# Moving one batch's input loads and folds to later steps of a fused FFT-filter and gated-FFN kernel

## The chip, the cores and the metric

The kernel runs on one core of one Trainium2 chip. Five engines work side by side, each in the order of its own instruction list: TensorE (PE) multiplies matrices, VectorE (DVE) and ScalarE (ACT) work element by element and take results out of PSUM, the accumulator memory, GpSimd (POOL) works element by element on SBUF, the on-chip memory, and SyncE (SP) issues transfers. POOL and ACT can issue transfers too. The metric is device time in microseconds (us); lower is better.

## The reference, cut to what matters

```python
X = np.fft.rfft(x, axis=1)                 # x: 8 batches, 3008 rows, 256 columns
Y = X * (filt_r + 1j * filt_i)[None]
y = np.fft.irfft(Y, n=3008, axis=1)
t = y.reshape(8 * 3008, 256)
out = (np.maximum(t @ w_gate, 0) * (t @ w_val)) @ w_out    # 256 -> 1536 -> 256
```

Each batch is Fourier transformed along its rows, multiplied by a filter, transformed back, and every row then goes through a gated feed-forward layer.

## The kernel before, in words

**The two halves.** The transform is split by 3008 = 94 x 32 into stages of small matmuls. For batches 2 to 7, one batch b goes through this chain:

1. *Chunk loads* (`load_chunk`). The batch's input comes in four chunks j = 0 to 3, each into its own part `XP[j]` of the tiles `XF`. One chunk is six transfers: four of 96 KB and two of 256 KB. They are issued by SP (`nc.sync`) or by POOL (`nc.gpsimd`); a POOL load is preceded by `hold_gpsimd`, a small copy that makes POOL wait for the feed-forward work of its step.
2. *Folds* (`fold_chunk`). Six POOL instructions per chunk form sums and differences, in place in `XP[j]`.
3. *`tiled_a`*. 32 matmuls per chunk into `psF`, copied to `asb` by ACT and DVE and stored by SP to the DRAM buffer `Abuf`.
4. *`load_at_tiled`*. SP loads the whole stage back in another order, into the tile `at`.
5. *Forward blocks* (`fwd`, `product`, `add`). Six blocks per batch, in three pairs: matmuls into `psX`, products with the two filter tables on DVE (`tt`, `uu`), and sums of these on POOL (`pp`).
6. *Inverse* (`inv`). One per pair: matmuls into `psD`, copied to `dsb`, stored by SP to the DRAM buffer `Dbuf`.
7. *`load_d`* brings it back as `dCb`, and `item_c` makes from it the rows `yT` that the feed-forward layer reads.

The feed-forward half is the main loop: 47 blocks of 512 rows, with 12 steps each. A step of `gv` makes one of the 12 hidden slices (two matmuls each into `psV` and `psG`, a copy to `vsb` by ACT, a product by DVE), and `o_part` runs four matmuls of the previous block's output into `psO`. ACT copies these to `osb`, and SP stores them.

**What sets the order.** The order is written out by hand. Step s = 12k + ft is pass ft of block k. The dictionary `side` holds for each step the transform work done in it, and each engine and queue carries out its share in that order. For batch b, `end` is the step its times are counted from: 51 for batch 1, 123 for batch 2, 195 for batch 3, 267 for batch 4. Batch 2 has its `tiled_a` at steps 51, 56, 61, 66, its `load_at_tiled` at 70, its forward pairs at 79, 92 and 105, its adds from one to eight steps behind each of these, its inverses at 90, 103 and 116, its `load_d` at 121 and its first `item_c` at 128. Batch 3 has its `tiled_a` at 123, 128, 133 and 138 and its first forward pair at 151. Batch 1's `load_d` is at step 50.

**The lines that matter.** The lists `loads` and `folds` give the steps of the four chunk loads and the four folds of a batch; batch 2 has its own lists, and the others take theirs from `end`. For batch 3, these come to 53, 59, 78, 101 for the loads and 65, 72, 88, 114 for the folds. The condition in `next_x` says which chunks SP loads. It sends chunks 2 and 3 of batch 2 and chunks 0 and 1 of batch 3 to SP, the rest to POOL.

In the profile, chunk loads are lines 333 and 337, folds 346 to 351, `tiled_a` 360 (matmuls), 367 (copies) and 370 (stores), `load_at_tiled` 378, `fwd` 396, `product` 413, `add` 423 and 424, `inv` 436, its stores 453, `load_d` 481, `item_c` 503, the feed-forward matmuls 520 and 541, and output stores 565.

Of the kernel before, what the change touches and what calls it, by code (L numbers as in the profile page):

```python
# [116 lines left out]
def kernel(  # L117
# [138 lines left out]
    def hold_gpsimd(tile_):  # L256

        scr = sb.tile([128, 8], FP32, tag="scr", bufs=2)
        nc.gpsimd.tensor_copy(scr[:tile_.shape[0]], tile_)  # L259
# [68 lines left out]
    def load_chunk(b, j, eng):  # L328

        xp = XP[j]  # L330
        for q in range(4):
            r, o = 32 * q, 8 * q + 2 * j
            eng.dma_start(xp[r:r + 24, 0:4:2, :],  # L333
                              _ap(x, (b * N1 * N2 + o) * D,
                                  [[N2 * D, 24], [47 * N2 * D, 2], [1, 512]]))
        for i in range(2):
            eng.dma_start(xp[:, 2 * i + 1, :],
                              _ap(x, ((b * N1 + 46 + 47 * i) * N2 + 2 * j) * D,
                                  [[8 * D, 4], [-N2 * D, 32], [1, 512]]))

    def fold_chunk(b, j):

        xp = XP[j]
        t = fs.tile([128, 2, 512], FP32, tag="fold", bufs=1, name="fold")
        tt = nc.gpsimd.tensor_tensor
        tt(t, xp[:, 0:2], xp[:, 2:4], op=ALU.add)  # L346
        tt(xp[:, 2:4], xp[:, 0:2], xp[:, 2:4], op=ALU.subtract)  # L347
        tt(xp[:, 1], xp[:, 2], xp[:, 3], op=ALU.add)
        tt(xp[:, 2], xp[:, 2], xp[:, 3], op=ALU.subtract)
        tt(xp[:, 0], t[:, 0], t[:, 1], op=ALU.add)  # L350
        tt(xp[:, 3], t[:, 0], t[:, 1], op=ALU.subtract)
        fold[b, j] = (xp[:, 0], xp[:, 3], xp[:, 1], xp[:, 2])

    def tiled_a(b, j):

        banks = [bank("psF", 2, D) for _ in range(4)]
        for c in range(4):
            for q in range(4):
                r = 32 * q
                nc.tensor.matmul(banks[q][32 * c:32 * c + 32], WF[r:r + 24, c, :],  # L360
                                 fold[b, j][c][r:r + 24], start=True, stop=True,
                                 tile_position=(r, 32 * c))
        asf = sb.tile([128, NC2 * D], BF16, tag="asb", bufs=3, name="asb")
        asf = asf.rearrange("p (n q d) -> p n q d", n=2, d=D)
        for q in range(4):
            copy = nc.scalar.copy if q % 2 == 0 else nc.vector.tensor_copy
            copy(asf[:, :, q, :], banks[q])  # L367
            done(banks[q])
        for c in range(4):
            nc.sync.dma_start(_ap(Abuf[b], ((48 * (c % 2) + 24 * (1 - c // 2)) * N2 + 8 * j) * D,  # L370
                                  [[N2 * D, 24], [1, 8 * D]]),
                              asf[32 * c:32 * c + 24])

    def load_at_tiled(b):

        ats[b] = sb.tile([128, NG, D], BF16, tag="at", bufs=1, name="at")
        for rr in range(4):
            nc.sync.dma_start(ats[b][32 * rr:32 * rr + 32],
                              _ap(Abuf[b], (48 * (rr % 2) + 24 * (rr // 2)) * N2 * D,
                                  [[D, 32], [N2 * D, 24], [1, D]]))  # L380
# [6 lines left out]
    def fwd(b, i):  # L387

        for e in range(2):
            psXs[b, i, e] = bank("psX", 2, D)  # L390
            left[b, i, e] = 2
        for r in range(2):
            for c in range(4):
                for e in range(2):
                    j = 4 * i + c
                    nc.tensor.matmul(psXs[b, i, e][32 * c:32 * c + 32, r],  # L396
                                     F2[64 * e:64 * e + 64, j, 32 * r:32 * r + 32],
                                     ats[b][64 * e:64 * e + 64, j, :] if b > 1 else ats[b][64 * e:64 * e + 64, :, j, :],
                                     start=True, stop=True, tile_position=(64 * e, 32 * c))

    def product(b, i, e, k, pool=False):

        psX = psXs[b, i, e]
        pool_, bufs, dt = (fs, 3, FP32) if b else (pro, 8, BF16)
        p = pool_.tile([128, 2, D], dt, tag=("tt", "uu")[k], bufs=bufs, name=("tt", "uu")[k])
        filt = (Ftr, Fti)[k][:, 2 * i + e, :]
        filt = dataclasses.replace(filt, ap=[list(filt.ap[0]), [0, 2], list(filt.ap[1])])
        if pool:
            xs = pro.tile([128, 2, D], FP32, tag="xs", bufs=3)
            nc.scalar.copy(xs, psX)  # L410
            nc.gpsimd.tensor_tensor(p, xs, filt, op=ALU.mult)
        else:
            nc.vector.tensor_tensor(p, psX, filt, op=ALU.mult)  # L413
        tus[b, i, e, k] = p
        left[b, i, e] -= 1
        if not left[b, i, e]:
            done(psX)

    def add(b, i, e):

        tt, uu = (tus.pop((b, i, e, k)) for k in range(2))
        p = tus[b, i, e, 0] = fs.tile([128, 2, D], BF16, tag="pp", bufs=6, name="pp")
        nc.gpsimd.tensor_tensor(p[:, 0], tt[:, 0], uu[:, 1], op=ALU.subtract)  # L423
        nc.gpsimd.tensor_tensor(p[:, 1], tt[:, 1], uu[:, 0], op=ALU.add)  # L424
# [50 lines left out]
    def load_d(b):  # L475

        for z in range(NZ):
            i = 8 * (NZ * b + z) % 48
            dCs[b, z] = dCb[:NROW, i:i + 8, :]
            for e in range(2):  # L480
                nc.sync.dma_start(dCs[b, z][48 * e:48 * e + 48],
                                  _ap(Dbuf[b], (64 * e + 16 * z) * NG * D,
                                      [[D, 48], [48 * D, 8], [1, D]]))
# [166 lines left out]
    def at_step(s, f):  # L650
        side.setdefault(s, []).append(f)
# [4 lines left out]
    for b in range(1, B):  # L656
        end = (b * S // W - 1) * NFT + C_AT[0] - 5
        starts, gap = ((-37, -25, -13), 4) if b == 1 else ((-44, -31, -18), 5)
        if b > 1:
            loads, folds = (((6, 12, 20, 30), (22, 34, 46, 46)) if b == 2 else  # L660
                            ([end - 72 + v for v in (-70, -64, -45, -22)], [end - 72 + v for v in (-58, -51, -35, -9)]))
            for j, e in enumerate((-72, -67, -62, -57)):
                def next_x(b=b, j=j):
                    if b == 2 and j > 1 or b == 3 and j < 2:
                        return load_chunk(b, j, nc.sync)
                    hold_gpsimd(prods[-1][:, 0:8])
                    load_chunk(b, j, nc.gpsimd)
                at_step(loads[j], next_x)
                at_step(folds[j], lambda b=b, j=j: fold_chunk(b, j))
                at_step(end + e, lambda b=b, j=j: tiled_a(b, j))  # L670
            at_step(end + e + 4, lambda b=b: load_at_tiled(b))
        for z, l in enumerate(starts):
            for i in (2 * z, 2 * z + 1):
                at_step(end + l, lambda b=b, i=i: fwd(b, i))
                for h in range(4):
                    s = end + l + i % 2 * gap + h
                    at_step(s, lambda b=b, i=i, h=h: product(b, i, h // 2, h % 2))
                    if h % 2:
                        at_step(s, lambda b=b, i=i, h=h: add(b, i, h // 2))

            def back(b=b, z=z, s=end + l + 6 + gap):
                rest = inv(b, z)
                if b == 1:
                    rest()
                else:
                    at_step(s + 1, rest)
            at_step(end + l + 6 + gap, back)
        at_step(end - (1 if b == 1 else 2), lambda b=b: load_d(b))
# [43 lines left out]
```

## Time and profile before

| | |
|---|---|
| Median of 3 runs | 880.95 us (879.96 to 882.09) |
| Profiled execution | 881.05 us |
| Its span, first to last instruction | 879.3 us |
| Busy in the span | PE 98%, DVE 66%, ACT 57%, POOL 54% |
| DMA | 101.62 MB, mean 116 GB/s |
| Granted PE clock, mean of the span | 0.994 of full |

The profile shows one execution. In its rows, a group is named by its source line, its engine, its operation and "output<-input"; "SPq" and "POOLq" are the issue queues of SP and POOL. A timeline row gives the start, the time from there to the end of the last of its instructions, and the count; the part in brackets is the time the engine stood idle before it and what ended that idle time. In an issue row the time is that of issuing, not of moving the data. A row of waits gives the total, how often, and the longest. PE is in-order and its instructions overlap a little, so that starts are a better guide than lengths. A granted clock of 1.00 is full speed, 0.50 half.

### The profile page before, as it was taken

Reading aid. Unit: us, or ns where it says so; the run is one execution under the profiler, and the core shown is the slowest. Engines: PE = TensorE matmul, PEld = TensorE weight load, DVE = VectorE, ACT = ScalarE, POOL = GpSimd, SP = SyncE. Lnnn points to the kernel's source line nnn. Section 1 sums busy time; section 2 is a strip of 40 time slices with the busy share of each in tenths; the row PEclk is TensorE's granted clock in tenths of the full one; section 3 lists DMA queues with packets and bytes.
Section 4 is the critical chain, followed back from the end, with each engine's and each line's share of the span. In section 5 each row is a group of like instructions: output and inputs, shape, how many; then the busy total and the mean of one; then the engine's idle time right before and its main releaser. Section 6 shows DMA issues by size and latency. Waiting matters only on the chain.

```text
span 879.3 us, 20548 instructions
## 1 busy us (share of the span) xinstructions
PE 860.3 (98%) x7709; PEld 500.1 (57%) x7709; DVE 581.9 (66%) x860; ACT 496.8 (57%) x903; POOL 471.2 (54%) x515
## 2 busy tenths in 40 slices
PE   8899999699999999999999999999999999999997
PEld 3345655365556565566655556555655565666665
DVE  3788865387665885577755777657865578655553
ACT  4775566255655556655655555555555555555553
POOL 7837895665677756868549576487660032100001
PEclk9999999799999999999999999999999999999999
DMA  9796364724467246562377433874444522511111
GB/s 234 182 191 141 103 137 136 164 57 101 120 184 140 70 98 151 165 142 56 96 188 171 97 89 90 205 151 103 83 110 114 121 54 60 123 36 35 38 32 54
DMA packets 103262, 101.62 MB, mean 116 GB/s; under 512 B 22411, under 2 KB 90539, under 8 KB 102394
## 3 DMA queue, kind: packets, MB, share of 16 engines
q1 hardware_dynamic: 82970, 76.78, 35.7%
q0 software_dynamic: 19792, 22.74, 12.1%
q8 instruction: 61, 1.00, 0.5%
q10 hardware_dynamic: 400, 0.79, 0.3%
q14 instruction: 39, 0.32, 0.1%
HBM read 58.23 MB, written 45.88 MB: 118 GB/s over the span
## 4 chain that ended last, share of the span: by engine, by line
PE 94%; DMA 3%; DVE 1%; ACT 1%; POOL 1%; issue 0%; SPq 0%; DVEq 0%
PE psV L520 28%; PE psG L520 27%; PE psO L541 27%; PE psF L360 3%; PE psY L503 3%; PE psA L267 2%; PE psD L436 2%; DMA XF<-in_x_dram 2%; PE psX L396 1%; DMA at<-Abuf 1%; DVE tt L413 0%; POOL out_dram L565 0%; DMA Abuf<-asb 0%; ACT AS L445 0%; DVE at L294 0%
## 5 line engine op out<-in xcount | busy, mean ns | idle before, releaser
L525 DVE SCALAR_TENSOR_TENSOR prod<-psG,vsb 128x512 bf16<-128x512 f32 x564 | 388.8, 691 | 237.7 <-ACT vsb L523 231.0
L523 ACT CAST vsb<-psV 128x512 bf16<-128x512 f32 x564 | 332.0, 589 | 234.0 <-PE psV L520 223.9
L541 PE MATMUL psO<-WoT,prod 128*128 128x256 bf16 x2256 | 336.9, 273 | 0.0
L520 PE MATMUL psV<-yT,WvT 128*128 128x512 bf16 x1128 | 336.8, 380 | 0.0
L520 PE MATMUL psG<-yT,WgT 128*128 128x512 bf16 x1128 | 336.2, 380 | 0.0
L541 PEld LDWEIGHTS <-prod 128*128 128x128 bf16 x2256 | 220.9, 98 | 144.1 <-issue 1.1
L520 PEld LDWEIGHTS <-WgT 128*128 128x128 bf16 x1128 | 110.2, 98 | 134.3 <-issue 1.1
L423 POOL TENSOR_TENSOR pp<-tt,uu 128x256 bf16<-128x256 f32 x84 | 61.1, 727 | 182.7 <-DVE uu L413 105.3
L520 PEld LDWEIGHTS <-WvT 128*128 128x128 bf16 x1128 | 100.4, 98 | 33.7 <-issue 22.0
L509 ACT CAST yT<-psY 128x512 bf16<-128x512 f32 x93 | 54.7, 588 | 42.8 <-PE psY L503 42.5
L413 DVE TENSOR_TENSOR tt<-psX,Ftr 128x512 f32<-128x512 f32 (+1 forms) x96 | 65.2, 684 | 11.2 <-PE psX L396 9.6
L554 ACT COPY osb<-psO 128x512 f32<-128x512 f32 x92 | 53.9, 586 | 23.8 <-PE psO L541 22.4
L565 POOL DMA_DIRECT2D out_dram<-osb x5 | 2.6, 536 | 119.4 <-ACT osb L554 119.4
L346 POOL TENSOR_TENSOR fold<-XF 128x1024 f32<-128x1024 f32 x24 | 56.4, 2352 | 11.1 <-DMA Abuf<-asb 9.4
L424 POOL TENSOR_TENSOR pp<-tt,uu 128x256 bf16<-128x256 f32 x84 | 61.0, 726 | 0.0
L413 DVE TENSOR_TENSOR uu<-psX,Fti 128x512 f32<-128x512 f32 (+1 forms) x88 | 59.9, 681 | 0.0
L347 POOL TENSOR_TENSOR XF<-XF 128x1024 f32<-128x1024 f32 x24 | 56.4, 2351 | 1.9
L333 POOL DMA_DIRECT2D XF<-in_x_dram x80 | 48.4, 609 | 1.9 <-issue 1.4
L367 ACT CAST asb<-psF 128x512 bf16<-128x512 f32 x48 | 25.8, 589 | 34.5 <-PE psF L360 34.5
L367 DVE CAST asb<-psF 128x512 bf16<-128x512 f32 x48 | 30.9, 686 | 18.2 <-PE psF L360 18.2
L259 POOL CAST scr<-prod 128x8 f32<-128x8 bf16 x20 | 3.8, 190 | 71.2 <-DVE prod L525 59.1
L503 PEld LDWEIGHTS <-dCb 96*128 96x128 bf16 (+1 forms) x604 | 33.3, 98 | 10.3 <-issue 6.8
(69 smaller groups left out, 483.1 us busy)
## 6 DMA issues: line engine op xcount, KB each, us to landing
Dbuf<-dsb SPq DMA_DIRECT2D x84, 128.0 KB
dCb<-Dbuf SPq DMA_DIRECT2D x56, 192.0 KB
XF<-in_x_dram POOLq DMA_DIRECT2D x40, 256.0 KB, 8.0
Abuf<-asb SPq DMA_DIRECT2D x96, 96.0 KB
at<-Abuf SPq DMA_DIRECT2D x24, 384.0 KB
XF<-in_x_dram POOLq DMA_DIRECT2D x80, 96.0 KB, 5.4
XF<-in_x_dram SPq DMA_DIRECT2D x28, 256.0 KB
out_dram<-osb SPq DMA_DIRECT2D x69, 94.0 KB
```

The costliest lines, as they stand in the source:

```text
L346: tt(t, xp[:, 0:2], xp[:, 2:4], op=ALU.add)
L347: tt(xp[:, 2:4], xp[:, 0:2], xp[:, 2:4], op=ALU.subtract)
L367: copy(asf[:, :, q, :], banks[q])
L413: nc.vector.tensor_tensor(p, psX, filt, op=ALU.mult)
L423: nc.gpsimd.tensor_tensor(p[:, 0], tt[:, 0], uu[:, 1], op=ALU.subtract)
L424: nc.gpsimd.tensor_tensor(p[:, 1], tt[:, 1], uu[:, 0], op=ALU.add)
L503: nc.tensor.matmul(psY[:, o:o + w], dCs[b, n2 // 8][:, n2 % 8, h * 128:(h + 1) * 128], M1[:, 1, n1:n1 + w] if b == 0 else M1[:NROW, 0, n1: ...
L509: nc.scalar.copy(dst, psY)
L520: nc.tensor.matmul(pt[:, :W], w[:, h, ft * 128:(ft + 1) * 128], yt[:, h, :], start=(h == 0), stop=(h == 1))
L523: nc.scalar.copy(vsb, psV[:, :W])
L525: nc.vector.scalar_tensor_tensor(prod, in0=psG[:, :W], scalar=0.0, in1=vsb, op0=ALU.max, op1=ALU.mult)
L541: nc.tensor.matmul(psO[:, t % 2], prods[ft][:, t * 128:(t + 1) * 128], WoT[:, ft, :], start=(ft == 0), stop=(ft == NFT - 1))
```

## The change

For batch 3, the steps of the chunk loads become 78, 87, 98, 110 in place of 53, 59, 78, 101. Those of the folds become 88, 101, 114, 122 in place of 65, 72, 88, 114. SP now loads chunks 1, 2 and 3 of batch 3, and POOL chunk 0; before, SP loaded 0 and 1, and POOL 2 and 3. Other batches keep their steps and their queues.

```diff
         if b > 1:
             loads, folds = (((6, 12, 20, 30), (22, 34, 46, 46)) if b == 2 else
+                            ((78, 87, 98, 110), (88, 101, 114, 122)) if b == 3 else
                             ([end - 72 + v for v in (-70, -64, -45, -22)], [end - 72 + v for v in (-58, -51, -35, -9)]))
             for j, e in enumerate((-72, -67, -62, -57)):
                 def next_x(b=b, j=j):
-                    if b == 2 and j > 1 or b == 3 and j < 2:
+                    if b == 2 and j > 1 or b == 3 and j > 0:
                         return load_chunk(b, j, nc.sync)
                     hold_gpsimd(prods[-1][:, 0:8])
                     load_chunk(b, j, nc.gpsimd)
```

## The prediction

> **What bounds the kernel now.** I read the page first, then TensorE's waits, the chain around the longest of them, and a table by stage. A "step" is one pass of the main loop, number 12k + ft.
>
> ```profile
> span 879.3 us, 20548 instructions
> PE 860.3 (98%) x7709; PEld 500.1 (57%) x7709; DVE 581.9 (66%) x860; ACT 496.8 (57%) x903; POOL 471.2 (54%) x515
> PE 94%; DMA 3%; DVE 1%; ACT 1%; POOL 1%; issue 0%; SPq 0%; DVEq 0%
> ```
>
> TensorE (PE) is busy for 98% of the span and carries 94% of the chain. A change that touches no matmul can only pay, or cost, where PE stands still or runs slowly. Its waits are few:
>
> ```profile
> PE psX L396 <- DMA at<-Abuf: 7.3, 2, 4.1
> PE psA L267 <- DMA XF<-in_x_dram: 3.1, 3, 1.6
> ```
>
> The second row is the start of the program. The first is in the middle, and it is in the stretch that the change edits:
>
> ```profile
> 161.64 0.60 PE L541 MATMUL psO<-WoT,prod 128*128 128x256 bf16 x4
> 165.46 0.39 PE L396 MATMUL psX<-at,F 64*32 64x256 bf16 x1 [3.22 <-DMA at<-Abuf]
> 169.94 1.05 PE L396 MATMUL psX<-at,F 64*32 64x256 bf16 x31 [4.09 <-DMA at<-Abuf]
> 170.92 1.04 PE L520 MATMUL psV<-yT,WvT 128*128 128x512 bf16 x2
> 175.99 0.59 PE L520 MATMUL psV<-yT,WvT 128*128 128x512 bf16 x2
> ```
>
> This is step 79, batch 2's first forward blocks, waiting for `at` (the batch's stage-A result, loaded back from DRAM at step 70). The wait is 3.22 + 4.09 = 7.31 us, and behind it the same pair of matmuls takes 1.04 where it later takes 0.59. What that is worth together is read from the same stretch of four batches, first `tiled_a` to first inverse; columns are the stretch, its length, busy times of PE, PEld, DVE, ACT and POOL, granted PE clock, DMA share, GB/s:
>
> ```profile
> 120.14:188.09 67.95, 60.64 (x518) 33.94 (x526) 36.82 (x56) 33.15 (x60) 43.73 (x38) 0.92 0.58 137
> 235.84:293.42 57.58, 57.58 (x520) 32.89 (x528) 36.71 (x56) 33.08 (x60) 38.44 (x42) 1.00 0.63 154
> 341.13:398.69 57.56, 57.56 (x519) 32.83 (x526) 36.73 (x56) 33.07 (x60) 38.43 (x42) 1.00 0.67 159
> 446.49:504.04 57.55, 57.55 (x519) 32.82 (x526) 36.73 (x56) 33.04 (x60) 38.40 (x42) 1.00 0.66 159
> ```
>
> Batches 3, 4 and 5 need 57.55 to 57.58 us for the same matmuls at clock 1.00; batch 2 needs 67.95 at 0.92. The excess is 67.95 - 57.58 = 10.37 us: 7.31 of standing still and 3.06 of slow clock. It is the only excess of its kind.
>
> **Why `at` is late.** SP's queue, batch 2 and then batch 3, and DMA by single microseconds (the last two columns are share and GB/s):
>
> ```profile
> 131.57 2.13 SPq L333 DMA_DIRECT2D XF<-in_x_dram  x4
> 133.76 1.19 SPq L337 DMA_DIRECT2D XF<-in_x_dram  x2
> 137.24 6.11 SPq L565 DMA_DIRECT2D out_dram<-osb  x4
> 143.52 1.59 SPq L333 DMA_DIRECT2D XF<-in_x_dram  x4
> 145.16 1.19 SPq L337 DMA_DIRECT2D XF<-in_x_dram  x2
> 155.29 1.54 SPq L370 DMA_DIRECT2D Abuf<-asb  x4
> 158.90 2.93 SPq L378 DMA_DIRECT2D at<-Abuf  x4
> ...
> 261.99 1.52 SPq L370 DMA_DIRECT2D Abuf<-asb  x4
> 265.90 2.55 SPq L378 DMA_DIRECT2D at<-Abuf  x4
> ...
> SPq L565 <- DMA XF<-in_x_dram: 9.4, 4, 2.7
> ...
> 143.64 1.07 PE psF L360 x32
> 259.39 1.07 PE psF L360 x32
> ...
> 159.00:160.00 1.00, 1.00 (x8) 0.68 (x7) 0.57 (x1) 0.72 (x2) 0.92 (x2) 1.00 0.06 19
> 160.44 9.37 DMA at<-Abuf
> 275.00:276.00 1.00, 1.00 (x8) 0.54 (x6) 0.69 (x1) 0.72 (x3) 0.00 (x0) 1.00 0.78 157
> 276.00:277.00 1.00, 1.00 (x8) 0.69 (x7) 0.53 (x1) 0.44 (x1) 0.00 (x0) 1.00 0.24 79
> ```
>
> In batch 3 the last Abuf stores are issued 261.99 - 259.39 = 2.60 us after the last `tiled_a` and `at` 265.90 - 259.39 = 6.51 us after it. In batch 2 these are 155.29 - 143.64 = 11.65 and 158.90 - 143.64 = 15.26: 9 us later. The two XF rows are batch 3's chunks 0 and 1 (steps 53 and 59). They put 12 issues (3.4 and 2.8 us) into SP's queue, and the output stores behind them wait another 9.4 us for XF transfers. With everything in order on SP, the last Abuf stores and `at` inherit that. In batch 3 the next batch's chunks are issued by POOL in the same steps, and nothing is late.
>
> **The change, part by part.** (a) *Two SP loads leave steps 53 and 59.* SP then carries in this stretch what it carries in batch 3. `at` should go out at 143.64 + 6.51 = 150.15. Its flight: 158.90 to 160.44 + 9.37 = 169.81 is 10.9 us here; in batch 3 the transfer fades in the 275 and 276 rows, some 10.1 to 10.9 after its issue. So it lands at 160.3 to 161.1, against PE's readiness at about 161.64 + 0.43 = 162.07. I take the stall as gone with 1 to 1.8 us to spare: -10.37 us. Bounds: the whole 10.37, or, if SP still is some 3 us late from `load_d` of batch 1, a wait of about 2 us that stays, with no slow clock worth naming: -8.
>
> On the slow part, the Trainium skill ("TensorE: Matmul & The Clock Gate", Part 1) says that an idle window of about 3.4 us halves the clock and about 3.4 us of busy time restores it. By that the slow part is worth an estimated 1.7 us and the time would be about 872; the trace has 3.06, which decides.
>
> (b) *POOL at step 78.* It issued chunk 2 there and now issues chunk 0, with the same hold and the same six transfers: 0. Its load at step 101 goes, about 4 us of POOL. Rows for it and the folds:
>
> ```profile
> 186.71 2.35 POOL L346 TENSOR_TENSOR fold<-XF 128x1024 f32<-128x1024 f32 x1
> 195.37 1.27 POOL L351 TENSOR_TENSOR XF<-fold 128x512 f32<-128x512 f32 x1
> 204.86 0.72 POOL L424 TENSOR_TENSOR pp<-tt,uu 128x256 bf16<-128x256 f32 x1
> 213.56 0.72 POOL L423 TENSOR_TENSOR pp<-tt,uu 128x256 bf16<-128x256 f32 x1 [4.07 <-PE psG L520]
> 220.34 0.73 POOL L423 TENSOR_TENSOR pp<-tt,uu 128x256 bf16<-128x256 f32 x1 [2.46 <-DVE uu L413]
> 222.94 0.73 POOL L423 TENSOR_TENSOR pp<-tt,uu 128x256 bf16<-128x256 f32 x1 [1.19 <-DVE uu L413]
> 225.52 0.64 PE L436 MATMUL psD<-pp,I2t 32*64 32x256 bf16 x32
> 240.16 0.19 POOL L259 CAST scr<-prod 128x8 f32<-128x8 bf16 x1 [5.94 <-DVE prod L525]
> 277.23 0.19 POOL L259 CAST scr<-prod 128x8 f32<-128x8 bf16 x1 [3.50 <-DVE prod L525]
> ```
>
> (c) *Folds.* One fold is six instructions, 186.71 to 195.37 + 1.27: 9.9 us. All times from here on are on the clock of before. Step 88 keeps a fold, of another chunk. Step 101's is new: it would run 205.6 to 215.5 between the adds of pairs 2 and 3, so the first add of pair 3 slides from 213.56 by 2 us; an add pair takes 1.4 us and the third waits for DVE until 220.34, so POOL has caught up there, well before the inverse at 225.52: 0. Step 114 keeps one. Step 122's is new: 234.2 to 244.2, holding batch 4's first POOL load back from 240.16 by 4 us; POOL has 3.5 us idle ahead of 277.23 and more between batch 3's adds: 0. The two folds taken away at steps 65 and 72 covered nothing.
>
> (d) *SP loads at steps 87, 98, 110.* Each is 2.8 to 3.4 us of issue, plus up to the 6.11 us in which the stores behind it hung. They come some 16 us apart where the two of before came 12 apart. Behind them stand output stores, the Dbuf stores and `load_d`:
>
> ```profile
> 229.16 1.72 SPq L453 DMA_DIRECT2D Dbuf<-dsb  x4
> 233.13 6.68 SPq L481 DMA_DIRECT2D dCb<-Dbuf  x8
> ...
> 244.52 0.42 PE L503 MATMUL psY<-M,dCb 96*128 96x8 bf16 x7
> ...
> 121.60 4.03 SPq L481 DMA_DIRECT2D dCb<-Dbuf  x8
> L503 PEld LDWEIGHTS <-dCb x192: 95/97/152, 128.8 to 388.0; 96*128 96x128 bf16 x182, 128*128 128x128 bf16 x10
> ```
>
> Step 110 is at about 216 (counting steps of 1.3 us back from 225.52), so the last Dbuf stores have 13 us for the load's 3.4 + 6.1: on time. If not, batch 1's `dCb` was read 128.8 - 121.60 = 7.2 us after its issue, so `load_d` may slip 244.52 - 233.13 - 7.2 = 4.2 us unseen. I take 0; as a bound, a slip like the 9 us above, less 3.5 and 4.2, costs about 1.5 us.
>
> **Sum.** PE's own order of instructions is the same in both kernels. The profiled execution is 881.05 us (span 879.3 plus 1.75 around it); 881.05 - 10.37 = 870.7. That execution stands 0.1 above the median of 880.95, so I forecast 870.6. About 0.2% (1.8 us) can be told from no change.
>
> **Rivals.** (1) *Part of the wait stays.* SP is not quite on time, or `at` flies longer than 11 us. The spare time of 1 to 1.8 us speaks for it, three later batches without a wait against. Gain 6 to 8: 873 to 875.
> (2) *Bytes, not the queue.* If `at` were late because the 16 DMA engines were full, moving the issue would mend little: about 881. The 159 row speaks against it: with `at` still unissued, the engines were 0.06 busy. The Trainium skill ("DMA: Bandwidth & Descriptors", Issuing engines are not separate DMA queues) says that a choice of issuing engine saves only sequencer time, usually a small share; that row shows a case where the sequencer's place is what is short.
> (3) *The new SP loads make `dCb` late,* as in (d): 872 to 873; at twice that slip, with slow clock, some 877.
> (4) *Slower: POOL stalls in front of the adds.* The fold of chunk 1 at step 101 stands ahead of pair 3's adds in POOL's order. If its load has not landed, POOL waits and the inverse of step 116 with it. Fold starts up to about 209 cost nothing (four add pairs of 1.4 us behind it end before 225.5); each later microsecond stalls PE, with 3 us of slow clock on top. It takes a stall of 7.3 us, so a fold start near 217, to eat the gain, and more to be slower: 883 for a start at 219. Step 87 is at about 183.5, so the load would have to take 33 us; the longest wait behind an SP load here cleared by 143.35, 11.8 us after its 131.57 issue.
>
> **How the numbers follow.** Full gain 0.78 (own range 869.5 to 872); (1) 0.08; (2) 0.03; (3) 0.05; (4) and anything slower 0.06. Faster is full, (1) and (3): 0.91; same 0.03; slower 0.06. The range 869.3 to 874.0 takes in the full gain, a spread of a microsecond as between the runs, and most of (1) and (3).
>
> **What would show it.** Right: no wait of psX on `at` at step 79, which starts near 162; clock 1.00 there; the stretch from batch 2's first `tiled_a` to its first inverse near 57.6; `at` issued near 150; all later stages at their old lengths, about 10.4 earlier. Wrong: a wait of psX above 1 us; psD waiting for POOL at steps 103 or 116; psY waiting for `dCb` at step 128; or a batch other than 2 with a stretch above 58.

## The result

The changed kernel takes 872.42 us (median of 6 runs, 871.88 to 874.61) against 880.74 us for the kernel before (6 runs, 878.59 to 882.09). The ratio is 0.9911, 95% interval 0.9894 to 0.9927: 8.3 us, or 0.9%, faster. The profiled execution took 872.1 us, its span 870.0.

From TensorE's waits in the changed kernel, which fill seven rows, the longest and the only one of psX (in the views of this part, rows that the text does not need are left out):

```profile
PE psA L267 <- DMA XF<-in_x_dram: 1.6, 3, 0.8
...
PE psX L396 <- DVE at L294: 0.8, 1, 0.8
```

The row that carried the prediction, psX waiting for the transfer `at<-Abuf`, is gone. All seven belong to the start of the program, before the main loop. The table by stage, with the same columns as before, for the stretch from first `tiled_a` to first inverse of batches 2 and 3:

```profile
120.14:177.72 57.58, 57.13 (x504) 32.81 (x510) 36.82 (x56) 33.05 (x60) 24.48 (x26) 1.00 0.61 137
225.47:283.05 57.58, 57.16 (x506) 32.88 (x512) 36.71 (x56) 33.08 (x60) 46.43 (x48) 1.00 0.64 155
```

Batch 2 now needs 57.58 us where it needed 67.95, at clock 1.00 where it had 0.92. (This trace lacks some matmul records, so PE's busy time reads a little low.) SP's queue shows why, in rows that answer to those of steps 61 to 70 before:

```profile
146.38 1.53 SPq L370 DMA_DIRECT2D Abuf<-asb  x4
149.31 2.94 SPq L378 DMA_DIRECT2D at<-Abuf  x4
171.74 3.43 SPq L333 DMA_DIRECT2D XF<-in_x_dram  x4
218.91 1.72 SPq L453 DMA_DIRECT2D Dbuf<-dsb  x4
222.90 6.53 SPq L481 DMA_DIRECT2D dCb<-Dbuf  x8
```

The last Abuf stores go out at 146.38 in place of 155.29, and `at` at 149.31 in place of 158.90. The last `tiled_a` starts at 143.77 in this execution, so `at` is 5.54 us behind it; before it was 15.26. The loads now stand behind `at`, from 171.74 on. The last Dbuf stores and `load_d` come 10.25 us earlier than before, as the rest of the program behind batch 2's stall does.

### The profile page after: what moved, and what is told of

Same layout as the page of the kernel before. It is cut to its first block, busy times and chain, and to the rows that moved or that the text cites. A ratio compares the mean times of both kernels' runs of the same rounds, so it can differ in the third digit from the quotient of the medians.

```text
span 870.0 us, 20431 instructions
## 1 busy us (share of the span) xinstructions
PE 850.7 (98%) x7587; PEld 498.9 (57%) x7709; DVE 581.9 (67%) x860; ACT 496.7 (57%) x903; POOL 467.0 (54%) x508
## 4 chain that ended last, share of the span: by engine, by line
PE 90%; DVE 3%; DMA 2%; ACT 2%; issue 1%; POOL 1%; ACTq 0%; DVEq 0%
PE psG L520 29%; PE psO L541 27%; PE psV L520 26%; PE psF L360 3%; PE psY L503 2%; DVE prod L525 2%; PE psD L436 2%; PE psA L267 1%; ACT vsb L523 1%; PE psX L396 1%; DVE tt L413 1%; DMA Ftr<-in_filt_r_dram 1%; DMA XF<-in_x_dram 1%; POOL Ftr L237 0%; DMA Fti<-in_filt_i_dram 0%
## 5 line engine op out<-in xcount | busy, mean ns | idle before, releaser
L520 PE MATMUL psG<-yT,WgT 128*128 128x512 bf16 x1113 | 332.1, 379 | 5.7
L520 PE MATMUL psV<-yT,WvT 128*128 128x512 bf16 x1023 | 313.3, 379 | 0.1
L333 POOL DMA_DIRECT2D XF<-in_x_dram x76 | 45.8, 608 | 1.4 <-issue 0.9
L503 PEld LDWEIGHTS <-dCb 96*128 96x128 bf16 (+1 forms) x604 | 33.0, 97 | 10.2 <-issue 6.8
```

What stands on the lines that cost most here:

```text
L520: nc.tensor.matmul(pt[:, :W], w[:, h, ft * 128:(ft + 1) * 128], yt[:, h, :], start=(h == 0), stop=(h == 1))
```

## The experiments

Three theories run through the expectations. Theory A: `at` is late because of its place in SP's queue, behind two chunk loads. Theory B: it is late because of the bytes of these loads on the DMA engines, whoever issues them. Theory C: POOL's folds at steps 65 and 72 hold up something that `at` needs.

All kernels here differ from one of the two kernels above in a few lines. The table gives for each: how long after batch 2's last `tiled_a` matmuls `at` was issued; how long psX then waited for it at step 79; and what batches 2 and 3 lost. A loss is the time from a batch's first `tiled_a` matmul to that of the next batch, less 105.3 us, which is what it takes in an undisturbed batch. These come from the profiled execution of each kernel, the medians and ratios from all runs. A ratio is taken against runs of the kernel before from the same round; their medians were 880.4 to 881.8 us, so that medians of different rounds compare to about a microsecond only. The start of the program alone varies by more: the first `tiled_a` of batch 2 comes at 118.9 to 121.8 us in these kernels, with nothing edited ahead of it. And from batch 4 on single batches lose up to 0.5 us, so that losses of this size say nothing.

| kernel | `at` issued | psX waits | batch 2 loses | batch 3 loses | median us | ratio to before (95%) |
|---|---|---|---|---|---|---|
| before | 15.3 | 7.3 | 10.4 | 0 | 880.74 | |
| changed | 5.5 | 0 | 0 | 0 | 872.42 | 0.9911 (0.9894 to 0.9927) |
| folds only | 15.0 | 7.1 | 9.3 | 0 | 882.15 | 1.0013 (0.9989 to 1.0036) |
| one early, SP | 8.2 | 0.2 | 0.5 | 0.2 | 873.02 | 0.9901 (0.9883 to 0.9919) |
| one early, POOL | 5.5 | 0 | 0 | 0 | 873.05 | 0.9916 (0.9901 to 0.9931) |
| tiny early, SP | 6.3 | 0 | 0 | 0 | 871.76 | 0.9906 (0.9889 to 0.9922) |
| all by POOL | 13.1 | 5.0 | 7.4 | 0 | 876.45 | 0.9945 (0.9925 to 0.9966) |
| behind at, SP | 5.6 | 0 | 0 | 0 | 872.22 | 0.9905 (0.9890 to 0.9920) |
| behind at, POOL | 5.5 | 0 | 0 | 0 | 872.14 | 0.9902 (0.9887 to 0.9917) |
| old queues | 5.6 | 0 | 2.0 | 3.8 | 874.88 | 0.9929 (0.9903 to 0.9955) |
| late chunk 1 | 5.7 | 0 | 1.1 | 3.9 | 874.39 | 0.9934 (0.9920 to 0.9949) |
| bunched loads | 5.6 | 0 | 0 | 0 | 872.23 | 0.9906 (0.9889 to 0.9923) |
| late chunk 3 | 5.6 | 0 | 0 | 0 | 873.74 | 0.9918 (0.9903 to 0.9933) |

### The folds alone

```diff
 (in the kernel before)
+                            ((53, 59, 78, 101), (88, 101, 114, 122)) if b == 3 else
```

> Only the folds of batch 3 move to 88, 101, 114, 122; its loads keep their steps and queues. Theories A and B: at is as late as before, wait of psX about 7.3 us, 879 to 882 us. Theory C: the wait goes, 871 to 873 us.

TensorE's wait and SP's `at` in this kernel:

```profile
PE psX L396 <- DMA at<-Abuf: 7.1, 2, 4.2
...
153.86 1.55 SPq L370 DMA_DIRECT2D Abuf<-asb  x4
157.44 2.56 SPq L378 DMA_DIRECT2D at<-Abuf  x4
```

Nothing is gained: 882.15 us. Theory C falls, and the gain belongs to the loads.

### One early load, by SP and by POOL

```diff
 (in the kernel before; first by SP, then by POOL)
+                            ((53, 87, 98, 110), (88, 101, 114, 122)) if b == 3 else
-                    if b == 2 and j > 1 or b == 3 and j < 2:
+                    if b == 2 and j > 1 or b == 3 and j in (0, 1, 2, 3):      # by POOL: (1, 2, 3)
```

> The changed kernel, but SP loads chunk 0 at step 53, ahead of at; the other three loads and all folds as in the changed kernel. Theory A: SP is late by about 8 us at step 59 but has no second load there and recovers most of it by step 66, so at is issued 0 to 4 us later than 149.3 and psX waits 0 to 3 us; 872 to 875 us. Theory B: half the bytes, about half the wait (3.7 us) and some slow clock, 876 to 878 us.

> As the experiment with one early load on SP, but POOL issues it: chunk 0 at step 53 by POOL, the rest as in the changed kernel. Same bytes, other queue. Theory A: at is issued 5.5 to 6.5 us after batch 2's last stage-A matmuls (the early load on SP had 8.2, the changed kernel 5.5), no wait, 872 to 873 us. Theory B: as with SP, about 8 us after them, a wait of 0 to 1 us, 873 to 874 us. A further loss would have to come from POOL, which is 10 us behind at step 53.

SP's queue in the kernel with the early load on SP:

```profile
133.62 1.97 SPq L333 DMA_DIRECT2D XF<-in_x_dram  x4
139.03 6.13 SPq L565 DMA_DIRECT2D out_dram<-osb  x4
153.47 2.58 SPq L378 DMA_DIRECT2D at<-Abuf  x4
```

POOL's load, and SP's queue, in the kernel with the early load on POOL:

```profile
134.22 2.42 POOL L333 DMA_DIRECT2D XF<-in_x_dram  x4
134.38 1.69 SPq L565 DMA_DIRECT2D out_dram<-osb  x4
138.75 1.84 SPq L370 DMA_DIRECT2D Abuf<-asb  x4
149.36 2.89 SPq L378 DMA_DIRECT2D at<-Abuf  x4
```

The same bytes move at nearly the same time. In SP's queue they hold four output stores for 6.13 us in place of 1.69 and leave `at` 2.7 us later; in POOL's queue they do nothing to `at`, which goes out 5.5 us behind the last `tiled_a`, as in the changed kernel. They do slow the stores there. The traces hold the times at which transfers report that they have landed (the landings given below are read from them): the four Abuf stores issued from 138.75 on land after 5.7 to 6.2 us, where those issued from 138.70 on in the changed kernel take 1.8 to 2.2. But SP waits for them only 0.3 us longer than it does in the changed kernel. One chunk in SP's queue is just about absorbed (a wait of 0.2 us), as theory A had it. The two medians do not differ: nearly all of the 2.7 us of lateness fits into the slack.

### Issue slots or landing

```diff
 (in the changed kernel)
+                if b == 3 and j < 2:
+                    at_step((53, 59)[j], lambda b=b, j=j: load_chunk(b, j, nc.sync, 16))
 (and load_chunk takes the width, 16 elements here, 512 in the other loads)
```

This kernel does twelve small extra transfers whose data the full loads overwrite later.

> The changed kernel plus twelve extra transfers on SP at steps 53 and 59, shaped like the loads of chunks 0 and 1 of before but 16 elements wide in place of 512 (1/32 of the bytes; chunks 0 to 3 are loaded in full later, as in the changed kernel). If the twelve issue slots make at late: at more than 3 us later than in the changed kernel, psX waits 2 us or more, 875 us or more. If it is SP waiting for these transfers to land, which needs their bytes: at is at most 1 us late, no wait, 872 to 873.5 us.

```profile
136.91 1.39 SPq L565 DMA_DIRECT2D out_dram<-osb  x4
149.35 2.71 SPq L378 DMA_DIRECT2D at<-Abuf  x4
```

With the twelve issues there but only 1/32 of their bytes, the output stores behind the first load take 1.39 us in place of 6.11, and `at` is 0.7 us later than in the changed kernel. So the issue slots are not what makes SP late; it is SP waiting for loads to land. The traces show where: SP's transfers use eight completion marks in turn, and each waits for the one eight places ahead of it. In the kernel before, the output store that goes out at 140.09 us stands eight places behind the 256 KB load transfer of 133.76, which landed at 140.07. Six large loads in the list therefore stop the stores behind them until the loads have landed.

### All four chunks by POOL, at the old steps

```diff
 (in the kernel before)
-                    if b == 2 and j > 1 or b == 3 and j < 2:
+                    if b == 2 and j > 1 or b == 3 and j in ():
```

> Steps of loads and folds as before (53, 59, 78, 101 and 65, 72, 88, 114); only the queue differs: POOL issues all four chunks of batch 3. Theory A (at is late because SP's queue runs late behind two chunk loads): with the loads off SP, at is issued near 149 to 151, no wait of psX at step 79, about 871 to 873 us. Theory B (at is late because of the bytes of chunks 0 and 1 on the DMA engines): the same bytes move in the same stretch, so the wait of about 7 us and the slow clock stay, 879 to 882 us. Theory C (POOL's folds at steps 65 and 72 hold something that at needs): unchanged, 879 to 882 us.

POOL's two loads, SP's queue, SP's own waits for transfers from 140 to 157 us, DMA (the last two columns are share and GB/s) and TensorE's wait in this kernel:

```profile
133.58 2.42 POOL L333 DMA_DIRECT2D XF<-in_x_dram  x4
137.53 2.40 POOL L333 DMA_DIRECT2D XF<-in_x_dram  x4
...
142.48 5.04 SPq L565 DMA_DIRECT2D out_dram<-osb  x5
148.29 5.17 SPq L370 DMA_DIRECT2D Abuf<-asb  x4
156.18 2.60 SPq L378 DMA_DIRECT2D at<-Abuf  x4
...
SPq L565 <- DMA Abuf<-asb: 3.0, 1, 3.0
SPq L370 <- DMA Abuf<-asb: 2.7, 3, 1.1
SPq L378 <- DMA Abuf<-asb: 2.7, 1, 2.7
SPq L370 <- DMA out_dram<-osb: 1.9, 1, 1.9
...
144.00:148.00 4.00, 4.00 (x45) 2.35 (x30) 2.67 (x4) 2.96 (x6) 0.91 (x1) 1.00 1.02 176
...
167.03 1.05 PE L396 MATMUL psX<-at,F 64*32 64x256 bf16 x31 [3.92 <-DMA at<-Abuf]
```

The same stretch of the changed kernel:

```profile
SPq L378 <- DMA Abuf<-asb: 1.4, 1, 1.4
...
144.00:148.00 4.00, 3.95 (x56) 2.04 (x26) 2.95 (x5) 2.32 (x5) 0.00 (x0) 1.00 0.43 103
```

Theory A misses here. No chunk stands in SP's queue, and `at` is still issued at 156.18 and waited for, 5.0 us in all; the median is 876.45 us, with runs from 873.37 to 879.81. Theory B is not met either, since part of the gain is there. SP again waits for landings, but of its own stores: 10.3 us in the four rows, against 1.4 in the changed kernel. While both chunks are moving (DMA share about 1.0 from 140 to 152 us) the stores land late: the four Abuf stores issued from 138.06 on take 9.1 to 11.1 us. SP, which waits for the transfer eight places ahead, is late with them. POOL issues the two loads only 4 us apart because it is 10 us behind at step 53, from the folds of batch 2; SP had issued them 12 us apart. So this kernel differs from the one before in more than the queue, and how much of its wait is due to the bunching is not shown. One chunk, as above, did no harm.

### Loads behind `at`, by SP and by POOL

```diff
 (in the kernel before; first by SP, then by POOL)
+                            ((71, 72, 98, 110), (88, 101, 114, 122)) if b == 3 else
-                    if b == 2 and j > 1 or b == 3 and j < 2:
+                    if b == 2 and j > 1 or b == 3 and j in (0, 1, 2, 3):      # by POOL: (2, 3)
```

> The changed kernel, but SP loads chunks 0 and 1 at steps 71 and 72, directly behind the at load of step 70. Theory A (the place in SP's queue): at is issued on time, near 149, and only output stores and later work stand behind the loads; psX waits 0 to 1 us, 872 to 874 us. Theory B (bytes): 1.75 MB now share the DMA engines with at's own 1.5 MB, its flight grows from about 11 to 15 us or more, psX waits 3 to 6 us with slow clock, 876 to 881 us.

> The changed kernel, but POOL loads chunks 0 and 1 at steps 71 and 72, during the flight of at (with SP these loads were held until at had landed; POOL does not wait for SP's transfers). Chunks 2 and 3 on SP as in the changed kernel. If only SP's order matters: at goes out near 149, lands near 158, no wait, 872 to 873 us. If bytes matter by themselves: 1.75 MB beside at's 1.5 MB stretch its flight from 9 to 11 us to 14 to 18, psX at step 79 waits 2 to 6 us, with slow clock 875 to 881 us.

In the first kernel SP issued the loads only from 157.77 on, though their steps lie near 151, and `at` had landed at 158.66; it kept the order but could not test the bytes. In the second POOL issued the first chunk and two transfers of the second while `at` was flying, the rest from 161.85 on. SP's `at`, POOL's first load, a microsecond of DMA (the last two columns are share and GB/s), then psX:

```profile
149.59 2.63 SPq L378 DMA_DIRECT2D at<-Abuf  x4
...
153.06 2.41 POOL L333 DMA_DIRECT2D XF<-in_x_dram  x4
...
159.00:160.00 1.00, 1.00 (x8) 0.68 (x7) 0.39 (x2) 0.58 (x1) 0.00 (x0) 1.00 1.06 215
...
162.57 0.63 PE L396 MATMUL psX<-at,F 64*32 64x256 bf16 x32
```

The same microsecond in the changed kernel:

```profile
159.00:160.00 1.00, 1.00 (x8) 0.64 (x7) 0.44 (x1) 0.72 (x2) 0.00 (x0) 1.00 0.22 70
```

DMA is busier with the chunk behind it, but `at` lands at 160.35, 10.8 us after its issue, against 159.88 and 10.6 us in the changed kernel. I had expected 14 to 18 if bytes mattered. psX starts 18.5 us behind the last `tiled_a` in both, without a wait. The first of the load's transfers landed at 161.26, behind `at`. So loads that go out behind `at` landed behind it and cost it next to nothing; what bytes moving beside `at`, ahead of its landing, would do is tested by no kernel here. The medians of both kernels, 872.22 and 872.14, are those of the changed kernel: the loads may stand close behind `at`.

### The old queues at the new steps

```diff
 (in the changed kernel)
-                    if b == 2 and j > 1 or b == 3 and j > 0:
+                    if b == 2 and j > 1 or b == 3 and j in (0, 1):
```

> Steps of loads and folds as in the changed kernel, queues as before (SP loads chunks 0 and 1, POOL chunks 2 and 3). Theory A and theory B: nothing is ahead of at, so no wait at step 79; POOL spends about 4 us more on each of the loads at steps 98 and 110, which the adds behind them take up; 871 to 873 us, the same as the changed kernel within 1 us. If the three SP loads were what matters in the change, this would be slower than it by more than 1.5 us.

The expectation of "no difference" was wrong. TensorE's timeline, rows with a wait in batches 2 and 3 and rows behind the last; a microsecond behind that wait (the third column from the end is the granted clock); and SP's `at` of batch 3:

```profile
198.58 0.32 PE L436 MATMUL psD<-pp,I2t 32*64 32x256 bf16 x8 [0.53 <-POOL pp L423]
199.26 0.31 PE L436 MATMUL psD<-pp,I2t 32*64 32x256 bf16 x7 [0.36 <-POOL pp L424]
...
272.81 0.98 PE L396 MATMUL psX<-at,F 64*32 64x256 bf16 x31 [1.95 <-DMA at<-Abuf]
273.73 1.03 PE L520 MATMUL psV<-yT,WvT 128*128 128x512 bf16 x2
276.57 0.59 PE L520 MATMUL psV<-yT,WvT 128*128 128x512 bf16 x2
...
273.00:274.00 1.00, 1.00 (x32) 0.44 (x17) 0.59 (x1) 0.00 (x0) 1.00 (x4) 0.50 0.36 112
...
255.78 2.33 SPq L565 DMA_DIRECT2D out_dram<-osb  x5
262.17 2.53 SPq L378 DMA_DIRECT2D at<-Abuf  x4
```

A POOL load takes POOL about 4 us, and at steps 98 and 110 it stands ahead of the last adds of a pair, for which the inverse then waits: batch 2 loses 2.0 us. POOL's lateness also pushes batch 4's first load from 233.94 to 238.39, and batch 3's `at` is 10.0 us behind its last `tiled_a` in place of 6.7 and is waited for. The median is 2.5 us above that of the changed kernel, by the ratios 1.6 us, and the intervals of the two ratios overlap. The profiled execution, 877.7 us, was the longest of this kernel's, so that its 5.8 us of loss are more than the usual. By these rows the choice of SP for chunks 2 and 3 is a part of the gain; the medians alone do not show it.

### Chunk 1 loaded directly ahead of its fold

```diff
 (in the changed kernel)
-                            ((78, 87, 98, 110), (88, 101, 114, 122)) if b == 3 else
+                            ((78, 100, 104, 110), (88, 101, 114, 122)) if b == 3 else
```

> The changed kernel, but SP loads chunk 1 at step 100, directly ahead of its fold at 101, and chunk 2 at 104. If POOL waiting for a chunk stalls the adds behind it (the prediction's fourth rival): the load is issued near 193 and lands near 202 to 204, the fold starts then in place of 195.3, and pair 3's adds end 3 to 5 us too late for the inverse of step 116: psD waits 3 to 5 us, with slow clock, 876 to 880 us. If the slack on POOL is larger than worked out: 872 to 873 us.

```profile
200.66 2.36 POOL L346 TENSOR_TENSOR fold<-XF 128x1024 f32<-128x1024 f32 x1 [5.97 <-DMA XF<-in_x_dram]
...
215.41 0.32 PE L436 MATMUL psD<-pp,I2t 32*64 32x256 bf16 x8 [0.19 <-POOL pp L423]
216.10 0.31 PE L436 MATMUL psD<-pp,I2t 32*64 32x256 bf16 x7 [0.37 <-POOL pp L424]
...
PE psX L396 <- DMA at<-Abuf: 2.0, 1, 2.0
```

POOL stands for 5.97 us in front of the fold, which starts 6.0 us later than in the changed kernel (both counted from the first `tiled_a` of batch 2), and the inverse of step 116 waits for the adds as the fourth rival described, but for 0.6 us; batch 2 loses 1.1 us and not 3 to 5. The larger loss, 3.9 us, is again in batch 3, where `at` is 10.2 us behind its last `tiled_a`. This profiled execution, 876.04 us, too was the longest of its kernel.

### Is it the bunching of batch 4's loads?

```diff
 (in the changed kernel)
-                             ([end - 72 + v for v in (-70, -64, -45, -22)], ...
+                             ([end - 72 + v for v in ((-66 if b == 4 else -70), -64, -45, -22)], ...
```

> The changed kernel, with one other edit: batch 4's first chunk load, by POOL, at step 129 in place of 125, so that it goes out directly ahead of the second at 131. If two POOL loads back to back slow SP's transfers (the reading of the runs with all loads on POOL, with the old queues, and with the late chunk 1): batch 3's at goes out about 10 us after its last stage-A matmuls in place of 6.5, psX waits about 2 us in batch 3, its stretch loses about 4 us, 875 to 877 us. If those runs lost it on POOL's adds instead: nothing in batch 3, 872 to 873 us.

```profile
237.70 0.19 POOL L259 CAST scr<-prod 128x8 f32<-128x8 bf16 x1 [3.35 <-DVE prod L525]
241.73 0.20 POOL L259 CAST scr<-prod 128x8 f32<-128x8 bf16 x1
...
256.59 3.05 SPq L378 DMA_DIRECT2D at<-Abuf  x4
```

No: with the two loads 4.0 us apart in place of 5.5 and nothing else changed, `at` goes out 7.1 us behind the last `tiled_a`, and nothing is lost. Two loads back to back are not enough.

### Chunk 3 loaded directly ahead of the last Dbuf stores

```diff
 (in the changed kernel)
-                            ((78, 87, 98, 110), (88, 101, 114, 122)) if b == 3 else
+                            ((78, 87, 98, 116), (88, 101, 114, 122)) if b == 3 else
```

> The changed kernel, but SP loads chunk 3 at step 116, directly ahead of the last Dbuf stores of step 117. If the slack of the prediction's third rival is right (stores 3 to 9 us late, 4.2 us of them free): psY at step 128 waits 0 to 4 us for dCb, 872 to 876 us. POOL's fold at step 122 also waits for this chunk, so batch 4's first POOL load moves later and closer to the second, which by the reading of bunched loads delays batch 3's at as well, up to 4 us more: 876 to 879 us if both happen.

`load_d` is issued at 226.86, 0.5 us after batch 3's first `tiled_a` matmul, where the changed kernel has it 2.7 us ahead of that: 3.1 us late. No psY waits for it, which fits the 4.2 us of slack in the prediction. POOL's loads of batch 4 go out at 236.14 and 240.27, as early and as close as in the kernel with the late chunk 1 (235.90 and 239.94), and batch 3 loses nothing. The median is 873.74, 1.3 above the changed kernel's, by the ratios 0.6. The profiled span is 1.7 us longer, and none of that lies where the edit works: 0.8 is ahead of the first `tiled_a`, 0.4 in batches 4 and 6, 0.5 behind the last matmul.

So what makes `at` late in batch 3 in two kernels and not in two others with nearly the same POOL loads is not settled. In both, SP hangs for some microseconds on output or Abuf stores that land late. Three output stores of the same step (the second to fourth of their row) take 12.5 to 12.9 us to land with the old queues and 10.2 to 10.8 with the late chunk 1, against 3.9 to 4.7 with the bunched loads, 7.7 to 8.7 with the late chunk 3 and 5.2 to 7.8 in the changed kernel. With the late chunk 1 they go out behind the start of POOL's second load (242.98 against 240.17), with the bunched loads ahead of it (240.24 against 241.86), which would fit a store landing behind the load bytes issued ahead of it; no experiment changes only that.

## Why the prediction was right

**The stall and its price.** Right, and by the mechanism named. The excess of batch 2 went to zero, 67.95 to 57.58 us, wait and slow clock together. `at` was forecast for 150.15 and issued at 149.31; psX starts at 162.30 without a wait. The flight was 10.6 us, to 159.88, within the 10.1 to 10.9 taken. The slack, 162.30 - 159.88 = 2.4 us, is more than the 1 to 1.8 of the prediction, mainly because `at` went out 5.54 us behind the last `tiled_a` and not 6.51. The kernel with one early load on SP bears it out: `at` 2.7 us later, and a wait of 0.2.

**Why `at` was late.** Right in that the loads stood ahead of `at`, too simple in the working. The prediction counted the twelve issues and the stores hung behind them alike. The tiny loads show that the issues make `at` 0.7 us late, of 9.7; the landing of the loads is the rest. And the second rival was put too low: all four chunks on POOL leave SP's list as clean as in batch 3, and 5.0 of the 7.3 us of the wait remain. Nor would that rival have meant 881 us: the change takes the loads out of the stretch altogether, so it pays under both readings, and on this point the forecast was safe without the reason being settled. The 159 row shows that the engines were idle while `at` waited to be issued; it does not show that they had been idle when the stores ahead of it should have landed.

**POOL's side.** The timeline of POOL in the changed kernel:

```profile
195.28 2.35 POOL L346 TENSOR_TENSOR fold<-XF 128x1024 f32<-128x1024 f32 x1
205.19 0.72 POOL L423 TENSOR_TENSOR pp<-tt,uu 128x256 bf16<-128x256 f32 x1
233.94 0.20 POOL L259 CAST scr<-prod 128x8 f32<-128x8 bf16 x1
239.45 0.19 POOL L259 CAST scr<-prod 128x8 f32<-128x8 bf16 x1 [1.56 <-DVE prod L525]
```

With 10.37 subtracted, the prediction had the new fold from 195.2, the delayed adds from 205.1, and batch 4's load at 233.8. All three hold within 0.2 us, and no wait of TensorE comes of any of them. The margin behind the last is the 1.56 us in the last row.

**SP's side.** The Dbuf stores at 218.91 and `load_d` at 222.90 are where 229.16 and 233.13 less 10.37 put them; three SP loads cost nothing.

**The size.** 10.4 us was forecast, 8.3 measured between medians, 8.95 between the two profiled executions. The stage gave all of the 10.37. The span shrank by 879.3 - 870.0 = 9.3, and the 1.1 us between lies in places that the change does not touch: 0.13 at the start (first `tiled_a` at 120.27 against 120.14), 0.27 at one psX of batch 6 (0.90 us in place of 0.63), and 0.7 behind the last matmul, in the closing output stores, where POOL stood idle for 1.54 us; what made it idle was not found:

```profile
583.56 0.90 PE L396 MATMUL psX<-at,F 64*32 64x256 bf16 x32
862.34 2.13 POOL L565 DMA_DIRECT2D out_dram<-osb  x4 [1.54 <-issue]
```

Another 0.35 lies outside the span (2.1 against 1.75). The last 0.6 us, from 8.95 to 8.3, comes from comparing medians of six runs: the profiled execution of before lies 0.3 above its median, that of the changed kernel 0.3 below. The prediction took the excess of one execution as exact, and it varies: in the kernel with only the folds moved, whose `at` is late in the same way, batch 2 lost 9.3.

**The rivals.** The first, third and fourth did not come about. The fourth was tried, with a fold start 2.5 us past its bound (200.66, or 201.3 when counted from the changed kernel's first `tiled_a`, against 209 - 10.37 + 0.13 = 198.8). The prediction had each such microsecond as a stall, with 3 us of slow clock on top; psD waited 0.6 us and batch 2 lost 1.1, but batch 3 another 3.9. The prediction followed POOL's lateness to the next adds and not to the next batch's loads, and that is where it was dear.

**The clock.** The prediction said that a wait of 2 us would bring no slow clock worth naming. That was wrong. With the old queues, a wait of 1.95 us was followed by pairs of matmuls of 1.03 us in place of 0.59 until about 276.3, at a granted clock of 0.50, and batch 3 lost 3.8 us in all: the slow clock cost as much as the wait. With the late chunk 1 it came the same way behind a wait of 1.96 us. The Trainium skill ("TensorE: Matmul & The Clock Gate", Part 1) has an idle window of about 3.4 us ahead of the half clock; here less was enough, and the measurement decides. The estimate of 1.7 us for the slow clock worked out from it fits these two waits (3.8 less 1.95 is 1.9) better than the 3.1 behind the long wait of the kernel before.

## What to carry to other kernels

When the bounding engine is nearly full, look for the one stage that takes longer than its sisters: four batches with the same matmuls priced this change to within 2 us, and no average over the span showed it. A queue that waits for its own earlier transfers is late by what those take to land, not by what it takes to issue them, and loads from another queue can make them land late too; so put bulk loads behind a transfer that somebody waits for, not ahead of it. When work moves to a quieter place, check what the engine that now runs later was to start for the next batch.

## What the runs showed of the hardware that I had not expected

A wait of TensorE of 1.95 us was enough for the half clock: pairs at 1.03 to 1.06 us against 0.59 for the next 3.5 us, at a granted clock of 0.50. One chunk of 0.9 MB, issued by another engine ahead of the stores, made four Abuf stores land after 5.7 to 6.2 us in place of 1.8 to 2.2, without delaying `at`; two of them, 4 us apart, made it 9.1 to 11.1 us and held SP up, and in another batch and kernel did no harm. `at` itself flew 10.8 us with loads issued behind it and 10.6 without.
